# Moving the split of the second weights ahead of the next sum, and the first block's ELU ahead of a weight split, in a three-stage kernel on one core

## The chip, the cores and the metric

The kernel runs on one core of a Trainium2 chip. The metric is the device time of one execution in microseconds. Three executions of the kernel before took 698.92, 700.79 and 702.18 us, so the median is 700.79 us. The profile is of one more execution, of 699.52 us.

## The reference

Three stages follow each other. The first is an attention in which a query sees only the keys that fall to the same one of 16 centroids; there are 16 heads in all (2 batches of 8), 768 positions each. The second is a layer with an ELU between two products, for 1536 tokens. The third sends each token to one of eight experts. The change lies at the end of the first stage and in the second.

```python
def _moe_ref(x, w_in, w_out):            # x 1536 x 512, w_in 512 x 2048, w_out 2048 x 512
    h = x @ w_in
    g = np.where(h > 0.0, h, np.exp(np.minimum(h, 0.0)) - 1.0)
    return (g @ w_out).astype(np.float32)
```

## The kernel before

A product in full precision is made of three products of a reduced type: each operand is split into a head (names that end in H) and a rest (L), and head times head, rest times head and head times rest are summed in PSUM. For activations the head is a ScalarE copy and the rest a VectorE subtraction; for weights the head is a ScalarE copy (L705) and the rest a GpSimd subtraction (L706), both in `w_split`.

The weights of the second layer are taken as pairs of 32-bit words and rounded by a conversion, `round64`, one half of a 128 x 1024 tile `r` at a time. It is a generator whose steps are called from outside, one `next` each: ScalarE writes cv_a (L675) and then cv_t (L677), VectorE works cv_a (L679), cv_b (L681) and cv_b again (L684), and GpSimd sums cv_b and cv_t into r (L686). Half 0 of tile k holds first weights (w1), half 1 second weights (w2).

The second layer goes over the two batches, 16 steps each: k = 0 to 15 for the first batch, in which the weights are converted and also stored, and k = 16 to 31 for the second, in which they are read back. A step k has two blocks of hidden units times 384 tokens (part 0 and part 1, PSUM banks p and v). Each block takes twelve products on TensorE (L719, `ffn_h`): eight with w1H, then four with w1L. Then comes its ELU, `ffn_elu`, a generator of three steps: ScalarE makes two passes (L734, L735); VectorE one (L737) and ScalarE the head gH (L738); VectorE the rest gL (L740). Then come eighteen products with the second weights of the step before (L751, `ffn_second`): twelve with w2H and six with w2L. So step k needs r's half 1 of tile k - 1 (whose conversion began in step k - 1 as `high`), splits it into w2H and w2L, and prepares w1 of tile k + 1 (conversion `low`, begun in step k - 1).

The order on each engine is the order in which the code issues: the schedule is written out by hand, every engine works its own instructions strictly in that order, and semaphores join them. In a step the loop of `ffn` issues the end of `high` (a sum on GpSimd), the first block, the middle of `low` on VectorE, the first ELU's ScalarE passes, then the sum of `low` and the split of w2; later the second block, its ELU, and the split of w1 for the next step. In steps 9 to 14 GpSimd also finishes the last pair of heads, one piece per step (`side`: L501, L506 or L510).

The end of attention follows a written table, SCHEDULE, whose names W0 to W6 stand for parts of the second layer's step 0 that are put between the last pair's work: W0 to W3 issue three products each of the first block, W4 to W6 the three steps of its ELU (`elu[0]`). `early`, from `w_early`, is a generator of eleven steps that converts and splits the first weights of tiles 0 and 1; it is called after the last seven exponentials and at W0 to W3. Its last step sums r of tile 1 and splits it into w1H and w1L.

Of the kernel before, what the change touches and what calls it, by code (L numbers as in the profile page):

```python
# [65 lines left out]
class _Core:  # L66
# [446 lines left out]
    def steps(self):  # L513

        end = {}
        at = {"vtH": self.v_head, "vtL": self.v_rest, "loadqk": self.load_qk, "loadv": lambda n: self.load_nat(n + 1, "v"),
              "back": self.turn_back, "sv": self.similarities, "mx": self.largest, "eqsub": self.less_largest,
              "first": self.candidates, "least": self.first_of_them, "equal": self.one_hot, "rows": self.turn_one_hot,
              "oT": self.mask_rows}

        def put(at, name, f, *a):
            at[name] = lambda n: f(n, *a)
        for h in range(2):
            for nm in "qk":
                for x, f in (("turn", self.turn), ("TH", self.turn_head), ("raw", self.turn_raw), ("TL", self.turn_rest),
                             ("sim", self.similar)):
                    put(at, f"{x}{nm}{h}", f, nm, h)
            for name, f in (("back", self.turn_back), ("mx", self.largest), ("eqsub", self.less_largest),
                            ("first", self.candidates), ("least", self.first_of_them), ("equal", self.one_hot),
                            ("rows", self.turn_one_hot), ("oT", self.mask_rows)):  # L530
                put(at, f"{name}{h}", f, h)
            put(at, f"sT{h}", self.similar_out, h)
            put(at, f"moveT{h}", self.move_qk, h)
            put(at, f"moveO{h}", self.move_mask, h)
            for s in range(2 * self.NC):
                ab = "ab"[h]
                put(at, f"scores{s}{ab}", self.scores, s, h)
                put(at, f"flip{s}{ab}", self.flip, s, h)
                put(at, f"head{s}{ab}", self.head, s, h)
                put(at, f"rest{s}{ab}", self.rest, s, h)  # L540
        for s in range(2 * self.NC):
            put(at, f"peak{s}", self.peak, s)
            put(at, f"exp{s}", self.expo, s)
        for j in range(2 * self.NC // GU):
            for i in range(4):
                put(at, f"pv{j}{'abcd'[i]}", self.pv, j, i)
            put(at, f"pvlow{j}", self.pv_low, j)
            put(at, f"pvsum{j}", self.pv_sum, j)

        put(at, "invert", self.invert)  # L550
        for name, f in (("sumT", self.turn_sums), ("invrow", self.inverse_row), ("invdma", self.inverse)):
            put(end, name, f)
        for h in range(2):
            for x, f in (("mul", self.divide), ("xH", self.x_head), ("xL", self.x_rest)):
                put(end, f"{x}{h}", f, h)

        last = {}
        for i in range(4):
            put(last, f"W{i}", self.first_h, i)
        for i in range(4, 7):  # L560
            put(last, f"W{i}", lambda n: next(self.elu[0]))
        return at, end, last

    def first_h(self, n, i):

        self.ffn_h(0, 0, 3 * i, 3 * i + 3)
        next(self.early, None)

    def early_weights(self, u):
        NU, PER = self.B * self.H * self.NC, 2 * self.NC  # L570
# [189 lines left out]
    def ffn(self):  # L760

        NF = self.DFF // 128
        side = self.attention_rest()
        next(side)
        self.y, self.rest, low, high, routing = [], [], None, None, iter(())
        for k in range(2 * NF):
            if high:
                next(high, None)  # L770
            if k == 1:
                self.y.append(self.ffn_banks())
            if k == NF + 1:
                self.ffn_pools_after()
                routing = self.route_beside(0, self.y[0])
                next(routing)
                self.y.append(self.ffn_banks())
            if k:
                self.ffn_h(k, 0)
            if low:  # L780
                next(low)
                next(low)
                next(low)
            if k >= NF:
                self.w_split(k, 1)
                if k + 1 < 2 * NF:
                    self.w_split(k + 1, 0)
            elu, elu1 = self.elu[0] if k == 0 else self.ffn_elu(k, 0), self.ffn_elu(k, 1)
            next(elu, None)
            if low:  # L790
                next(low, None)
            if 0 < k <= NF:
                self.w_split(k - 1, 1)
            high = None
            if k < NF:
                high = self.round_half(k, 1)
                next(high)
            next(elu, None)
            self.ffn_h(k, 1)
            if high:  # L800
                next(high)
                next(high)
            next(elu, None)
            next(elu1)
            if high:
                next(high)
            if 0 < k < NF and k + 1 < 2 * NF:
                self.w_split(k + 1, 0)
            next(elu1)
            if high:  # L810
                next(high)
            next(elu1)
            low = None
            if k + 2 < NF:
                low = self.round_half(k + 2, 0)
                next(low)
                next(low)
            elif k + 2 < 2 * NF:
                self.w_load(k + 2)
            if k >= LATER:  # L820
                next(side, None)
            if k - NF in (4, 8):
                self.expert_load()
            ops = self.ffn_second(k - 1) if k else []
            for op in ops[:len(ops) // 2]:
                op()
            next(routing, None)
            for op in ops[len(ops) // 2:]:
                op()
            next(routing, None)  # L830
            if k:
                self.w_raw.pop(k - 1)
        self.drain(routing)
        for op in self.ffn_second(2 * NF - 1):
            op()
        self.rest.sort(key=lambda op: op[0])
# [555 lines left out]
```

## Time and profile before

| | |
|---|---|
| median of three executions | 700.79 us |
| the profiled execution | 699.52 us, span of the core 697.8 us |
| TensorE products busy | 666.6 us, 96% of the span |
| VectorE / ScalarE / GpSimd busy | 487.2 / 446.7 / 268.3 us |
| granted TensorE clock, mean | 0.984 of full speed |

The span is shorter than the execution's time by what lies before the first and after the last instruction. TensorE is busy for nearly the whole span, so most waits of the other engines cost nothing; what can be won on the way is the few gaps of TensorE. Busy shares of VectorE and GpSimd contain time in which an instruction has been issued and stands: an instruction's duration in a row runs from its issue to its end. In the timeline the start of an instruction can lie a little before the end of the one ahead of it on the same engine.

### The profile page before, as it was taken

The page shows a single profiled execution, that of the slowest core. Times are in us where ns is not written, and L with a number is a line of the kernel's source. Part 1 is how long each engine was busy: PE and PEld are TensorE (multiplying, and loading weights), DVE is VectorE, ACT ScalarE, POOL GpSimd, SP SyncE. Part 2 cuts the span into 40 slices and gives each one's busy share as a digit, 9 for nine tenths or more (in the row PEclk, how much of TensorE's full clock was granted, in tenths as well). Part 3 has the DMA queues.
Part 4 walks back from the last instruction along what each step waited for, and adds up shares of the span by engine and source line. Part 5 has one row for each costly group of instructions (what it writes and reads, how often), then busy time and mean ns, then how long its engine had stood idle before and what let it go on. Part 6 is the DMA issues. An engine that isn't in the chain of part 4 may idle for free. (4 is left out here: it accounts for less than half of the span.)

```text
span 697.8 us, 12196 instructions
## 1 busy us (share of the span) xinstructions
PE 666.6 (96%) x4272; PEld 608.7 (87%) x4272; DVE 487.2 (70%) x933; ACT 446.7 (64%) x968; POOL 268.3 (38%) x254
## 2 busy tenths in 40 slices
PE   5799999999999998999999999999999999999994
PEld 3699999999998887788888899999999898999994
DVE  5499998999999997999999852432364563226662
ACT  4499989899998987677767664445545312215551
POOL 1423446254545224666788752222243004022010
PEclk9699999999999999999999999999999999999998
DMA  7636657564664532655454446424110249989930
GB/s 174 156 77 141 157 130 162 127 142 114 152 141 102 126 116 62 210 192 192 168 195 161 172 173 214 160 73 166 62 61 16 91 172 378 339 290 316 354 141 13
DMA packets 73734, 111.41 MB, mean 160 GB/s; under 512 B 31105, under 2 KB 41441, under 8 KB 73664
## 3 DMA queue, kind: packets, MB, share of 16 engines
q1 hardware_dynamic: 70432, 106.07, 50.4%
q0 software_dynamic: 1488, 3.99, 1.6%
q8 instruction: 36, 0.59, 0.4%
q10 hardware_dynamic: 1744, 0.48, 0.3%
q14 instruction: 34, 0.28, 0.1%
HBM read 73.81 MB, written 16.92 MB: 130 GB/s over the span
## 5 line engine op out<-in xcount | busy, mean ns | idle before, releaser
L441 DVE TENSOR_TENSOR ptL<-ps_t,ptH 128x384 fp32r<-128x384 f32 x192 | 102.6, 551 | 10.4 <-ACT ptH L435 8.2
L435 ACT ACTIVATE ptH<-ps_t 128x384 fp32r<-128x384 f32 x192 | 91.2, 489 | 16.9 <-PE ps_t L423 12.8
L423 PE MATMUL ps_t<-ident,pe 128*128 128x128 f32 x576 | 94.3, 277 | 2.9 <-DVE ptL L441 2.2
L454 PE MATMUL ps_v<-ptH,vt 128*128 128x256 f32 x288 | 78.1, 295 | 0.0
L423 PEld LDWEIGHTS ps_t<-ident,pe 128*128 128x128 f32 x576 | 67.9, 141 | 11.6 <-DVE ptL L441 7.4
L454 PE MATMUL ps_v<-ptL,vt 128*128 128x256 f32 x288 | 77.2, 297 | 0.0
L706 POOL TENSOR_TENSOR w2L<-r,w2H 128x512 fp32r<-128x512 f32 x28 | 42.5, 1517 | 69.4 <-PE ps_t L751 62.2
L686 POOL TENSOR_TENSOR r<-cv_b,cv_t 128x512 int32<-128x512 int32 x32 | 43.1, 1346 | 44.6 <-DVE cv_b L684 24.2
L454 PEld LDWEIGHTS ps_v<-ptH,vt 128*128 128x128 f32 x288 | 54.0, 189 | 1.5
L454 PEld LDWEIGHTS ps_v<-ptL,vt 128*128 128x128 f32 x288 | 53.5, 190 | 0.2 <-DVE ptL L441 0.2
L407 DVE TENSOR_REDUCE st<-ps_sA 128x1 f32<-128x768 f32 x48 | 45.6, 949 | 8.4 <-PE ps_sA L401 8.0
L734 ACT ACTIVATE e<-ps_p 128x384 f32<-128x384 f32 x32 | 15.7, 490 | 55.7 <-PE ps_p L719 55.7
L407 DVE TENSOR_REDUCE st<-ps_sB 128x1 f32<-128x768 f32 x48 | 45.7, 952 | 4.3 <-PE ps_sB L401 4.2
L1197 POOL DMA_INDIRECT out_dram<-o,dest x10 | 11.5, 1155 | 92.1 <-DVE o L1195 91.5
L679 DVE SCALAR_TENSOR_TENSOR cv_a<-cv_a,d 128x512 f32<-128x512 f32 x32 | 44.3, 1383 | 3.5 <-ACT cv_a L675 3.3
L737 DVE SCALAR_TENSOR_TENSOR ps_p<-e,ps_p 128x384 f32<-128x384 f32 x32 | 17.9, 560 | 41.1 <-ACT e L735 41.1
L706 POOL TENSOR_TENSOR w1L<-r,w1H 128x512 fp32r<-128x512 f32 x32 | 44.1, 1379 | 6.4 <-ACT w1H L705 6.4
L414 ACT ACTIVATE pe<-ps_sA,st 128x768 f32<-128x768 f32 x48 | 43.3, 903 | 3.8 <-DVE st L407 3.8
L719 PE MATMUL ps_p<-xH,w1H 128*128 128x384 f32 x128 | 43.9, 343 | 2.0 <-DVE gL L740 2.0
L414 ACT ACTIVATE pe<-ps_sB,st 128x768 f32<-128x768 f32 x48 | 43.0, 897 | 0.5 <-DVE st L407 0.3
L719 PE MATMUL ps_p<-xL,w1H 128*128 128x384 f32 x128 | 42.9, 335 | 0.0
L719 PE MATMUL ps_v<-xL,w1H 128*128 128x384 f32 x124 | 41.4, 334 | 0.0
(378 smaller groups left out, 1930.8 us busy)
## 6 DMA issues: line engine op xcount, KB each, us to landing
ew<-in_moe_w_dram SPq DMA_DIRECT2D x32, 1024.0 KB, 7.6
d<-in_moe_w_in_dram SPq DMA_DIRECT2D x16, 512.0 KB, 4.0
d<-in_moe_w_out_dram SPq DMA_DIRECT2D x16, 512.0 KB, 4.1
wf_d<-r SPq DMA_DIRECT2D x16, 512.0 KB, 2.8
r<-wf_d SPq DMA_DIRECT2D x16, 512.0 KB, 3.3
KA<-kH SPq DMA_DIRECT2D x32, 192.0 KB, 3.7
natq<-in_q_dram SPq DMA_DIRECT2D x16, 192.0 KB, 3.8
natv<-in_v_dram SPq DMA_DIRECT2D x16, 192.0 KB, 3.9
```

Of the source, the lines that this page charges most:

```text
L407: self.nc.vector.tensor_reduce(st, self.sc[u][:, :, 0:384], axis=AX.XY, op=ALU.max, negate=True)
L414: self.nc.scalar.activation(pe, self.sc.pop(u)[:, :, 0:384], AF.Exp, bias=self.peaks.pop(u), accum_out=self.sums[n][:, s:s + 1])
L423: self.nc.tensor.transpose(ps[:, 0, j * 128:j * 128 + 128], self.pe[u][:, half, j * 128:j * 128 + 128], self.ident)
L435: self.nc.scalar.activation(self.split(u, half)[0], self.tp[u, half][:, 0, 0:384].rearrange("p (c q) -> p c q", c=3), AF.Copy)
L441: self.nc.vector.tensor_tensor(l, self.tp.pop((u, half))[:, 0, 0:384].rearrange("p (c q) -> p c q", c=3), h.bitcast(F32), ALU.subtract)
L454: self.nc.tensor.matmul(self.vp[n, j], lhsT=self.vt[n][:, j // NG, c, :], rhs=t, start=(part == 0 and i == 0), stop=(part == 3 and i == 2 ...
L679: V.scalar_tensor_tensor(a, a, LEAST_HI, hi.bitcast(F32), ALU.is_ge, ALU.mult)
L686: G.tensor_tensor(out.bitcast(I32), b, t, ALU.add)
L706: self.nc.gpsimd.tensor_tensor(l, x, h.bitcast(F32), ALU.subtract)
L719: self.nc.tensor.matmul(ps, lhsT=w[:, c, :], rhs=x[:, c, :], start=(i == 0), stop=(i == 11))
L734: S.activation(e, ps, AF.Relu, scale=-1.0)
L737: V.scalar_tensor_tensor(ps, e, -1.0, ps, ALU.add, ALU.max)
```

## The change

Two places are written in another order; no instruction is added or removed. In `ffn`, the split of w2 is issued ahead of the sum of `low`. At the end of attention, the last step of `early` (sum, w1H, w1L of tile 1) is called at W5, behind the first two steps of the first block's ELU, and no longer at W3.

```diff
         for i in range(4, 7):
-            put(last, f"W{i}", lambda n: next(self.elu[0]))
+            put(last, f"W{i}", self.first_elu, i)
         return at, end, last
 
     def first_h(self, n, i):
 
         self.ffn_h(0, 0, 3 * i, 3 * i + 3)
-        next(self.early, None)
+        if i < 3:
+            next(self.early, None)
+
+    def first_elu(self, n, i):
+        next(self.elu[0])
+        if i == 5:
+            next(self.early, None)
...
             elu, elu1 = self.elu[0] if k == 0 else self.ffn_elu(k, 0), self.ffn_elu(k, 1)
             next(elu, None)
+            if 0 < k <= NF:
+                self.w_split(k - 1, 1)
             if low:
                 next(low, None)
-            if 0 < k <= NF:
-                self.w_split(k - 1, 1)
```

GpSimd in two steps of the loop, before. `r` with cv_b and cv_t is a sum; of the two sums in a row the first belongs to second weights (half 1), the second to first weights (half 0).

```order
L686 TENSOR_TENSOR r_4070<-cv_b_4252,cv_t_4253 128x512
L686 TENSOR_TENSOR r_4289<-cv_b_4291,cv_t_4292 128x512
L706 TENSOR_TENSOR w2L_4340<-r_4070,w2H_4339 128x512
L706 TENSOR_TENSOR w1L_4372<-r_4289,w1H_4371 128x512
L686 TENSOR_TENSOR r_4211<-cv_b_4344,cv_t_4345 128x512
L686 TENSOR_TENSOR r_4381<-cv_b_4383,cv_t_4384 128x512
L706 TENSOR_TENSOR w2L_4432<-r_4211,w2H_4431 128x512
L706 TENSOR_TENSOR w1L_4464<-r_4381,w1H_4463 128x512
```

The same two steps now:

```order
L692 TENSOR_TENSOR r_4070<-cv_b_4252,cv_t_4253 128x512
L712 TENSOR_TENSOR w2L_4339<-r_4070,w2H_4338 128x512
L692 TENSOR_TENSOR r_4289<-cv_b_4291,cv_t_4292 128x512
L712 TENSOR_TENSOR w1L_4372<-r_4289,w1H_4371 128x512
L692 TENSOR_TENSOR r_4211<-cv_b_4344,cv_t_4345 128x512
L712 TENSOR_TENSOR w2L_4431<-r_4211,w2H_4430 128x512
L692 TENSOR_TENSOR r_4381<-cv_b_4383,cv_t_4384 128x512
L712 TENSOR_TENSOR w1L_4464<-r_4381,w1H_4463 128x512
```

In each step w2L and the sum of the next first weights have changed places; ScalarE and VectorE keep their order in the loop.

ScalarE at the end of attention, before. `ps_p` is the first block's bank, `xtmp` and `row` belong to the last pair of heads, `cv_a` begins the next conversion.

```order
L435 ACTIVATE ptH_4105<-ps_t1_4122 128x3x128
L705 ACTIVATE w1H_4140<-r_4070 128x512
L734 ACTIVATE e_4160<-ps_p_4091 128x384
L735 ACTIVATE e_4160<-e_4160 128x384
L738 ACTIVATE gH_4161<-ps_p_4091 128x384
L463 ACTIVATE xtmp_4167<-ps_v_4144 64x256
```

The same place now:

```order
L435 ACTIVATE ptH_4105<-ps_t1_4122 128x3x128
L740 ACTIVATE e_4155<-ps_p_4091 128x384
L741 ACTIVATE e_4155<-e_4155 128x384
L744 ACTIVATE gH_4156<-ps_p_4091 128x384
L711 ACTIVATE w1H_4163<-r_4070 128x512
L463 ACTIVATE xtmp_4167<-ps_v_4139 64x256
```

The three passes of the ELU stand ahead of w1H; the copy xtmp still comes last.

GpSimd at the same place, before, where `xH` and `xL` are the split of an attention result of the pair before the last:

```order
L706 TENSOR_TENSOR w1L_4048<-r_3859,w1H_4047 128x512
L686 TENSOR_TENSOR r_4070<-cv_b_4072,cv_t_4073 128x512
L706 TENSOR_TENSOR w1L_4141<-r_4070,w1H_4140 128x512
L506 CAST xH_175<-xr_3455 128x384
L510 TENSOR_TENSOR xL_176<-xr_3455,xH_175 128x384
L510 TENSOR_TENSOR xL_174<-xr_3455,xH_173 128x384
```

And now:

```order
L712 TENSOR_TENSOR w1L_4048<-r_3859,w1H_4047 128x512
L506 CAST xH_175<-xr_3455 128x384
L510 TENSOR_TENSOR xL_176<-xr_3455,xH_175 128x384
L692 TENSOR_TENSOR r_4070<-cv_b_4072,cv_t_4073 128x512
L712 TENSOR_TENSOR w1L_4164<-r_4070,w1H_4163 128x512
L510 TENSOR_TENSOR xL_174<-xr_3455,xH_173 128x384
```

The sum and w1L of tile 1 have gone behind one xH and one xL; the second xL stays behind them.

## Rows read from the trace of the kernel before

**Rows 1.** Busy time of TensorE by stretch: us, busy, instructions, clock, DMA.

```profile
410.00:690.00 280.00, 277.17 (x1761) 0.99 0.51 183
```

**Rows 2.** Timeline, TensorE's weight loads that waited: start, duration, form, idle before.

```profile
274.72 0.19 PEld L719 LDWEIGHTS ps_p<-xH,w1H 128*128 128x128 f32 x1 [2.27 <-ACT cv_a L675]
...
283.70 0.30 PEld L751 LDWEIGHTS ps_sA<-w2L,gH 128*128 128x128 f32 x2 [1.40 <-POOL w2L L706]
...
342.93 0.30 PEld L751 LDWEIGHTS ps_sA<-w2L,gH 128*128 128x128 f32 x2 [0.34 <-POOL w2L L706]
...
395.78 0.30 PEld L751 LDWEIGHTS ps_sA<-w2L,gH 128*128 128x128 f32 x2 [0.73 <-POOL w2L L706]
```

**Rows 3.** Timeline of TensorE, a step of the layer's second half.

```profile
499.55 0.33 PE L719 MATMUL ps_v<-xH,w1H 128*128 128x384 f32 x1
...
501.63 0.39 PE L751 MATMUL ps_sA<-w2H,gH 128*128 128x512 f32 x1
...
507.81 0.33 PE L719 MATMUL ps_v<-xH,w1H 128*128 128x384 f32 x1
```

**Rows 4.** Timeline, one step of the layer's first half.

```profile
311.81 0.71 PEld L719 LDWEIGHTS ps_p<-xH,w1L 128*128 128x128 f32 x4
...
313.50 0.75 DVE L684 SCALAR_TENSOR_TENSOR cv_b<-cv_a,top,cv_b 128x512 int32<-128x512 int32 x1
...
313.83 0.62 ACT L705 ACTIVATE w2H<-r 128x512 fp32r<-128x512 f32 x1
...
314.48 1.30 POOL L686 TENSOR_TENSOR r<-cv_b,cv_t 128x512 int32<-128x512 int32 x1 [2.10 <-ACT w2H L705]
...
315.04 1.29 DVE L679 SCALAR_TENSOR_TENSOR cv_a<-cv_a,d 128x512 f32<-128x512 f32 x1 [0.31 <-ACT cv_a L675]
...
315.74 1.75 POOL L706 TENSOR_TENSOR w2L<-r,w2H 128x512 fp32r<-128x512 f32 x1
...
316.72 1.05 DVE L681 TENSOR_SCALAR cv_b<-cv_a 128x512 int32<-128x512 int32 x1
...
317.47 1.45 POOL L706 TENSOR_TENSOR w1L<-r,w1H 128x512 fp32r<-128x512 f32 x1
...
317.69 0.55 DVE L737 SCALAR_TENSOR_TENSOR ps_v<-e,ps_v 128x384 f32<-128x384 f32 x1
...
318.16 1.31 DVE L684 SCALAR_TENSOR_TENSOR cv_b<-cv_a,top,cv_b 128x512 int32<-128x512 int32 x1
...
319.55 1.29 POOL L686 TENSOR_TENSOR r<-cv_b,cv_t 128x512 int32<-128x512 int32 x1 [0.63 <-DVE cv_b L684]
```

**Rows 5.** Timeline, the end of attention.

```profile
267.94 0.88 PE L719 MATMUL ps_p<-xH,w1L 128*128 128x384 f32 x4
...
269.18 1.28 POOL L686 TENSOR_TENSOR r<-cv_b,cv_t 128x512 int32<-128x512 int32 x1 [6.03 <-DVE cv_b L684]
...
270.49 0.63 ACT L705 ACTIVATE w1H<-r 128x512 fp32r<-128x512 f32 x1 [2.20 <-POOL r L686]
...
271.20 1.29 POOL L706 TENSOR_TENSOR w1L<-r,w1H 128x512 fp32r<-128x512 f32 x1 [0.74 <-ACT w1H L705]
...
273.20 0.38 ACT L463 ACTIVATE xtmp<-ps_v 64x256 f32<-64x256 f32 x1
```

**Rows 6.** Lines of GpSimd: shapes, count, busy us, mean ns, idle before.

```profile
L501 POOL TENSOR_TENSOR xr<-xr,inv 128x384 f32<-128x384 f32 x16 | 17.3, 1085 | 45.0 <-DMA inv<-inv_d 45.0
...
L506 POOL CAST xH<-xr 128x384 fp32r<-128x384 f32 x16 | 9.0, 564 | 0.0
```

**Rows 7.** Timeline, two close meetings of VectorE and GpSimd.

```profile
18.28 0.36 DVE L343 TENSOR_TENSOR oh<-eq,mn 128x192 bf16<-128x192 f32 x1
18.30 1.19 POOL L264 TENSOR_TENSOR qL<-raw,qH 128x384 fp32r<-128x384 f32 x1
...
362.91 1.28 POOL L686 TENSOR_TENSOR r<-cv_b,cv_t 128x512 int32<-128x512 int32 x1
362.96 1.78 DVE L679 SCALAR_TENSOR_TENSOR cv_a<-cv_a,d 128x512 f32<-128x512 f32 x1
```

## The prediction

> **What bounds the kernel now.** I read the page's busy shares first, then the waits of TensorE in the stretch that the change touches, then one step of that stretch engine by engine. From 410 us on TensorE is busy 277.17 of 280.00 us [rows 1], so a microsecond won or lost before that shows in full at the end. The stretch that the change touches is the first half of the second layer, the fifteen loop steps k = 1 to 15 from about 275 to 406 us. There TensorE stops once in each step, in front of the six products that read w2L [rows 2]. From 283.70 to 342.93 are seven steps, 8.46 us each; from 342.93 to 395.78 six steps, 8.81 us each [rows 2]. In the second half the same 42 products, with nothing late, take 8.26 us from 499.55 to 507.81 [rows 3]. So TensorE is only 0.20 and 0.55 us per step short of its own pace.
>
> What holds it is a chain of VectorE and GpSimd that take turns [rows 4]. GpSimd sums r at 314.48 to 315.78; VectorE's L679 starts at 315.04 and ends only at 316.33, 0.55 after GpSimd. GpSimd's w2L is issued at 315.74 and ends at 317.49, 1.16 after L679's end. L681 ends 0.28 after that (317.77), w1L 1.15 after L681 (318.92), L684 0.55 after w1L (319.47), and the next sum starts 0.08 later. Bare, w1L takes 1.29 [rows 5] and L684 0.75 [rows 4]. One of the two engines always stands until the other has finished; the passes that read PSUM (L737, 0.55) do not take part. The chain closes on itself in 8.46 us and TensorE waits on it.
>
> The Trainium skill, SBUF — State Buffer, Who interferes with whom, says that a VectorE instruction with two SBUF inputs and a GpSimd instruction that reads SBUF exclude each other for the whole instruction, the one issued first going first. The rows agree on the exclusion, but GpSimd's data starts about 0.12 us before VectorE's recorded end (1.16 against a bare 1.29), so not for the whole instruction; with two such handovers in the new chain below, holding it to the end would add 0.25 us per step, and the sum would be near zero instead of minus 1.4.
>
> **The change, part by part.** First the end of attention. In front of step 0 ScalarE stands 2.20 us until GpSimd's sum ends (269.18 + 1.28), and only after w1H (270.49 to 271.12) does it start the first block's ELU, although that block's last products were issued at 267.94 and were done by 268.82 [rows 5]. VectorE's xr pass and then the rest gL come behind ScalarE's copy at 273.20, and TensorE restarts at 274.72, after 2.27 us of idle weight load [rows 2, 5]. With the ELU ahead of w1H, its passes fill the 2.20 us. Between w1H's end and the copy 2.08 us of ELU go away (273.20 minus 271.12); w1H itself comes about 0.47 later, since gH of the ELU ends near 271.06 by my addition of the same passes. That leaves 2.08 - 0.47 = 1.6 us. What is late next is the same chain (w1H, copy, VectorE, gL), so not all of the 2.27 goes. GpSimd does one xH and one xL earlier, in the time in which it waited for the sum; these are read only in the second half of the layer. Term: -1.6, with 0 and -2.2 as ends.
>
> Second, the first w2L. At 283.70 TensorE had waited 1.40 us for it [rows 2]. With w2L ahead of the sum it is started once w2H is there, two microseconds or so earlier: -1.3. But TensorE then meets w1L of the next step, which now stands behind w2L and the sum; by the same durations that gives 0.6 back at once. Together -0.7.
>
> Third, the steady step. w2L needs w2H, which ends at 314.45, and the sum r started at 314.48 [rows 4]: so w2L takes the sum's slot, ends near 315.8, and TensorE's wait for it is gone. But the sum now ends where w2L ended, near 317.5; w1H, which on ScalarE reads that sum and started 0.7 earlier before, comes behind it, and w1L behind w1H. Call the end of the sum R. VectorE's L681, held back by the sum, ends at R + 0.28, L737 follows, and L684 is issued at R + 0.67 (318.16 against 317.49 [rows 4]). ScalarE starts w1H 0.03 after the sum, takes 0.63, and GpSimd issues w1L 0.08 later (270.46, 270.49, 271.20 [rows 5]): R + 0.74. L684 is 0.07 us ahead. Taking it first, L684 runs its bare 0.75 to R + 1.42, and w1L ends 1.15 later, at R + 2.57. Now TensorE waits for w1L, in the middle of its first block. The new cycle: w1L to TensorE 0.05; from the first w1L load (311.81) to w2H's end 2.64; w2L 0.08 + 1.29; L679 0.55; sum 1.16; to w1L's end 2.57. Sum 8.34, against 8.46: -0.12 in each of seven steps, -0.8. TensorE's own 8.26 is the lower end.
>
> Fourth, the six steps from 342.93 in which GpSimd also does a piece of the last pair (L501 or L510, about 1.0 us, or the cast L506 at 0.5 [rows 6]). There the sum of the other half comes late, and w2H with it. The cycle: L679 0.55, the extra piece 0.9, L681 0.28, sum 1.16, w2H 0.66, w2L 1.37, L679 0.55, sum 1.16, to w1L's end 2.57: 9.2 us, or 8.7 with a cast. Mean (4 x 9.2 + 2 x 8.7) / 6 = 9.03 against 8.81: +0.22 x 6 = +1.3. Before, the piece was paid only in part, because w2L stood last in the chain. In the last step w1L is late once more: +0.2. Step 0 itself has the same order as the others but costs nothing new: its sum waits for VectorE, not for GpSimd's place.
>
> Sum: -1.6 - 0.7 - 0.8 + 1.3 + 0.2 = -1.6; the second xL now runs beside VectorE's L679 of step 0, which takes 0.2 back (the xr and L679 passes follow each other there), so -1.4. Against the profiled execution's own 699.52 us that is 698.1. The median shown is 700.79, 1.27 above that execution, so I forecast 699.4.
>
> **The rivals.** A second outcome: GpSimd goes first at that meeting. The 0.07 us is less than the 0.08 by which VectorE issues an instruction before the one ahead of it has ended (318.16 against 317.69 + 0.55 [rows 4]). Two close meetings in the trace went by issue: at 18.28 VectorE, 0.02 ahead, ran its 0.36 and GpSimd's took 1.19; at 362.91 GpSimd, 0.05 ahead, ran its 1.28 and VectorE's took 1.78 [rows 7]. But at neither was a VectorE instruction, issued over its predecessor, ahead. If w1L wins, L684 ends 1.16 later; the sum behind it and the first two passes of the next conversion slide, and the next step's L684 of the first half is then issued after w2L and stands behind it. That delays L737, gH, ScalarE's second ELU and so w1H. TensorE waits for w1H at the head of the block. The cycle: w1H to TensorE 0.06, a block of twelve 2.08 [rows 3], result and the two ELU passes and w2H about 2.05, w2L 1.4, L684 0.55, L737 0.5, then six ScalarE passes (gH, the conversion's second pass, the second ELU's two, w1H) about 2.5: 9.1 us. Each of seven steps then costs +0.62, or +4.3; the steps with extra pieces about +2, the first w2L gives back 0.9 instead of 0.6: in all +4.7, 705.5 us. It decides from the moment that w1L is issued, or served, 0.07 us earlier against L684, and once in that state the order holds itself, since both then follow from ScalarE. For it: the smallness of the lead. Against it: both meetings above.
>
> A third outcome: the chain has more slack than I give it, w1L does not hold TensorE, and the steps go at TensorE's pace: -0.20 x 7 - 0.55 x 6 - 1.4 - 1.6 = -7.7 at the utmost, and half of that, 697, as a likely size. For it: the 8.46 before held about 0.6 us in which neither engine used its turn. Against it: four GpSimd and six VectorE passes add up to 7.8 us per step and 8.8 with an extra piece, so the latter cannot go below what they take now.
>
> A fourth: a part of the gain does not come through, because the copy at 273.20 still sets gL, or because in the new order GpSimd starts its data at VectorE's recorded end and not 0.12 us ahead of it; the rest stands as forecast: about 701. For the second speaks only the page quoted above, against it each handover in [rows 4].
>
> **How the numbers follow.** Chances: forecast 0.52 (its own range 697.6 to 701.2), GpSimd first 0.31, TensorE's pace 0.11, fourth 0.06. What a measurement of this kernel can tell from no change is about 0.5%, 3.5 us: faster means below 697.3, slower above 704.3. Faster: the third outcome and the forecast's edge, 0.13. Slower: the second but for its low edge, and an edge of the first, 0.31. Same: 0.56. The range reaches from 696.5, which takes in half of the third, to 706.3, the top of the second.
>
> **What would show it.** In the changed profile TensorE's waits for w2L should be gone; in their place stand short waits (near 0.1 us) for w1L within the first block and a step of 8.3 to 8.4 us before the extra pieces, 9.1 to 9.2 with them. L684 of the second half must take 0.75 and w1L 1.8. If instead L684 takes 1.76 and w1L 1.29, TensorE waits for w1H and the step is 9.1, the second outcome. TensorE's restart after the first two blocks should come at about 273.1 instead of 274.72. A step of 8.26 throughout, or a step above 9.3, would make the prediction wrong in its mechanism.

## The result, and the profile after

The changed kernel takes 704.34 us (median of six executions, 703.06 to 705.73); the kernel before takes 700.50 us in the same comparison. The ratio is 1.0056 with a 95% interval of 1.0037 to 1.0075: slower, where 699.4 us and no difference were forecast. The execution profiled is of 703.93 us, with a span of 702.2 us. The change sets every line from 671 on six lower in the file: L684 is now L690, L686 is L692, L706 is L712, L705 is L711, L719 is L725, L737 is L743.

From 414 us on TensorE is as busy as before, so the loss lies ahead of that, as [rows 1] let expect (columns as there; the further ones are the other engines):

```profile
414.00:690.00 276.00, 273.75 (x1745) 251.92 (x1744) 124.22 (x336) 119.75 (x261) 60.76 (x51) 1.00 0.52 186
```

The end of attention went as worked out. The timeline of the changed kernel there, which answers to [rows 5]:

```profile
268.10 0.86 PE L725 MATMUL ps_p<-xH,w1L 128*128 128x384 f32 x4
...
270.67 0.49 ACT L744 ACTIVATE gH<-ps_p 128x384 fp32r<-128x384 f32 x1 [0.63 <-DVE ps_p L743]
...
271.06 0.62 ACT L711 ACTIVATE w1H<-r 128x512 fp32r<-128x512 f32 x1
...
271.71 0.38 ACT L463 ACTIVATE xtmp<-ps_v 64x256 f32<-64x256 f32 x1
```

The ELU's last ScalarE pass is done before w1H, and the copy xtmp comes 1.49 us earlier (273.20 before). TensorE restarts at 273.23; from the first block's last products that is 5.13 us, where it was 274.72 - 267.94 = 6.78. So 1.65 us is gained, with 1.6 forecast.

The loss is in the loop. TensorE's loads that waited (timeline of the changed kernel, weight loads; they answer to [rows 2]):

```profile
273.23 0.19 PEld L725 LDWEIGHTS ps_p<-xH,w1H 128*128 128x128 f32 x1 [0.63 <-ACT cv_a L681]
278.73 0.19 PEld L757 LDWEIGHTS ps_sA<-w2H,gH 128*128 128x128 f32 x1 [1.39 <-ACT w2H L711]
283.65 0.19 PEld L725 LDWEIGHTS ps_p<-xH,w1H 128*128 128x128 f32 x1 [0.97 <-ACT w1H L711]
...
304.22 0.19 PEld L725 LDWEIGHTS ps_v<-xH,w1H 128*128 128x128 f32 x1 [0.35 <-DVE gL L746]
310.90 0.19 PEld L725 LDWEIGHTS ps_p<-xH,w1H 128*128 128x128 f32 x1 [0.65 <-ACT w1H L711]
313.29 0.19 PEld L725 LDWEIGHTS ps_v<-xH,w1H 128*128 128x128 f32 x1 [0.34 <-DVE gL L746]
```

The waits for w2L are gone. In their place TensorE waits twice in each step, for w1H at the head of the first block and for gL ahead of the second, and from 304.22 to 313.29 a step is 9.07 us. The lengths of all fifteen steps, each from the first load of one second block (k = 1 to 15) to that of the next, from the same view of both kernels:

```
before   10.37 | 8.46 8.47 8.47 8.44 8.46 8.46 8.47 | 8.85 8.88 8.68 8.70 8.89 8.87 | 8.25
changed  10.79 | 9.08 9.10 9.07 9.07 9.08 9.07 9.07 | 9.24 9.15 8.66 8.66 9.15 9.17 | 8.26
sums: +0.42, +4.31 for the seven steps, +1.16 for the six with an extra piece, +0.01
```

In all +5.90; less the 1.65 at the restart that is +4.25, and the two spans differ by 4.4 (the other 0.15 lie ahead of the restart). The seven steps without an extra piece are the loss. One of them on VectorE, ScalarE and GpSimd (timeline of the changed kernel, which answers to [rows 4], and above it the loop's first step):

```profile
278.75 1.29 POOL L712 TENSOR_TENSOR w2L<-r,w2H 128x512 fp32r<-128x512 f32 x1 [1.09 <-ACT w2H L711]
278.78 1.81 DVE L690 SCALAR_TENSOR_TENSOR cv_b<-cv_a,top,cv_b 128x512 int32<-128x512 int32 x1
...
310.93 1.29 POOL L712 TENSOR_TENSOR w1L<-r,w1H 128x512 fp32r<-128x512 f32 x1 [1.72 <-ACT w1H L711]
310.95 1.82 DVE L690 SCALAR_TENSOR_TENSOR cv_b<-cv_a,top,cv_b 128x512 int32<-128x512 int32 x1
...
314.97 1.41 POOL L712 TENSOR_TENSOR w2L<-r,w2H 128x512 fp32r<-128x512 f32 x1 [0.83 <-ACT w2H L711]
315.26 1.67 DVE L690 SCALAR_TENSOR_TENSOR cv_b<-cv_a,top,cv_b 128x512 int32<-128x512 int32 x1
316.85 0.55 DVE L743 SCALAR_TENSOR_TENSOR ps_p<-e,ps_p 128x384 f32<-128x384 f32 x1
...
317.43 0.49 ACT L744 ACTIVATE gH<-ps_p 128x384 fp32r<-128x384 f32 x1 [1.97 <-DVE ps_p L743]
...
319.31 0.61 ACT L711 ACTIVATE w1H<-r 128x512 fp32r<-128x512 f32 x1
```

A meeting is a place in the step where a pass of GpSimd and one of VectorE come close; if they overlap, one stands until the other is nearly through. Each step has two, and GpSimd wins both. At 310.93 w1L is 0.02 us ahead of the second half's L690, which takes 1.82. At 314.97 w2L is 0.29 ahead of the first half's L690, which takes 1.67. Behind that one stands L743 and, through it, ScalarE, which idles 1.97 us before gH and gets to w1H only at 319.31. This is the second outcome of the prediction, with its signature: L690 near 1.8 at the w1L meeting, w1L 1.29, a wait for w1H, 9.1 us per step. What the prediction did not see is at the top of the fence: in the loop's first step w2L was issued 0.03 us ahead of the first half's L690, and the order is there from then on until the extra pieces begin.

### The profile page after: what moved, and what is told of

Same layout as the page of the kernel before. It is cut to its first block, busy times and chain, and to the rows that moved or that the text cites. A ratio compares the mean times of both kernels' runs of the same rounds, so it can differ in the third digit from the quotient of the medians.

```text
span 702.2 us, 12182 instructions
## 1 busy us (share of the span) xinstructions
PE 669.8 (95%) x4272; PEld 607.0 (86%) x4272; DVE 492.6 (70%) x933; ACT 448.3 (64%) x968; POOL 266.8 (38%) x254
## 5 line engine op out<-in xcount | busy, mean ns | idle before, releaser
L712 POOL TENSOR_TENSOR w2L<-r,w2H 128x512 fp32r<-128x512 f32 x28 | 37.1, 1325 | 80.0 <-PE ps_t L757 62.1
L712 POOL TENSOR_TENSOR w1L<-r,w1H 128x512 fp32r<-128x512 f32 x32 | 44.9, 1403 | 25.0 <-ACT w1H L711 25.0
L692 POOL TENSOR_TENSOR r<-cv_b,cv_t 128x512 int32<-128x512 int32 x32 | 45.3, 1416 | 21.3 <-DVE cv_b L690 16.9
L725 PE MATMUL ps_p<-xH,w1H 128*128 128x384 f32 x128 | 44.7, 349 | 2.6 <-ACT w1H L711 2.2
L690 DVE SCALAR_TENSOR_TENSOR cv_b<-cv_a,top,cv_b 128x512 int32<-128x512 int32 x32 | 45.5, 1422 | 0.5
L685 DVE SCALAR_TENSOR_TENSOR cv_a<-cv_a,d 128x512 f32<-128x512 f32 x32 | 43.9, 1373 | 2.5 <-ACT cv_a L681 2.5
L743 DVE SCALAR_TENSOR_TENSOR ps_p<-e,ps_p 128x384 f32<-128x384 f32 x32 | 17.8, 557 | 39.3 <-ACT e L741 39.3
L725 PE MATMUL ps_p<-xL,w1H 128*128 128x384 f32 x128 | 42.9, 335 | 0.0
```

The source lines that it names most:

```text
L685: V.scalar_tensor_tensor(a, a, LEAST_HI, hi.bitcast(F32), ALU.is_ge, ALU.mult)
L690: V.scalar_tensor_tensor(b, a.bitcast(I32), self.top2, b, ALU.bitwise_and, ALU.bitwise_or)
L692: G.tensor_tensor(out.bitcast(I32), b, t, ALU.add)
L712: self.nc.gpsimd.tensor_tensor(l, x, h.bitcast(F32), ALU.subtract)
L725: self.nc.tensor.matmul(ps, lhsT=w[:, c, :], rhs=x[:, c, :], start=(i == 0), stop=(i == 11))
L743: V.scalar_tensor_tensor(ps, e, -1.0, ps, ALU.add, ALU.max)
```

## The experiments

My theory at this point: the loop has two orders that hold themselves, one of 8.3 us per step in which VectorE's L690 goes first at both meetings (VectorE's order below) and one of 9.07 in which GpSimd does (GpSimd's order), and the close meeting of the first step chooses. (It is close, but falls the same way each time: w2L, or the first piece of it, is issued 0.01 to 0.04 us ahead there in every trace of a kernel with the swap.) Its rivals: the new order is slower in any case; or the ELU's move, not the swap, does it; or, as the prediction had it, the meeting of w1L with L690 chooses. Step lengths below are k = 1 to 15, taken as above, with | around the six extra-piece steps; ratios are to the kernel before in the same comparison.

**ELU move alone** (the two statements of `ffn` back in the old order).

```diff
-            if 0 < k <= NF:
-                self.w_split(k - 1, 1)
             if low:
                 next(low, None)
+            if 0 < k <= NF:
+                self.w_split(k - 1, 1)
```

> The ELU's move alone, the split of the second weights left where it was. Theory (two separate terms, the loss is in the loop): TensorE restarts after the first two blocks 1.6 us earlier than before, the loop keeps its 8.46 us steps, about 698.9 us against 700.5 before. Rival (the earlier start also shifts the engines of the loop against each other and costs there): steps other than 8.46 us, 700.5 us or more.

698.52 us, ratio 0.9985 (0.9972 to 0.9998). Steps 10.87, 8.46 8.49 8.47 8.47 8.46 8.47 8.47 | 8.87 8.85 8.72 8.70 8.85 8.85 | 8.26: the old steps, so the loss isn't the ELU's. TensorE restarts 5.15 us after the first block's last products (271.70 against 266.55), 1.63 less than before. Yet the gain is 1.0 us, since the first step is 0.50 longer: the wait for w2H has grown. The second xL is now issued just 0.01 us ahead of VectorE's next conversion pass (L685, L679 before), which stands behind it and takes 1.54 instead of 1.03; L687, L743, ScalarE's passes and w2H come later by it. Timelines, this kernel and then the one before:

```profile
271.49 1.01 POOL L510 TENSOR_TENSOR xL<-xr,xH 128x384 fp32r<-128x384 f32 x1
271.50 1.54 DVE L685 SCALAR_TENSOR_TENSOR cv_a<-cv_a,d 128x512 f32<-128x512 f32 x1
...
277.19 0.19 PEld L757 LDWEIGHTS ps_sA<-w2H,gH 128*128 128x128 f32 x1 [1.35 <-ACT w2H L711]
```

```profile
274.53 1.03 DVE L679 SCALAR_TENSOR_TENSOR cv_a<-cv_a,d 128x512 f32<-128x512 f32 x1
...
279.71 0.19 PEld L751 LDWEIGHTS ps_sA<-w2H,gH 128*128 128x128 f32 x1 [0.87 <-ACT w2H L705]
```

**Swap in the loop alone** (the kernel before with the two statements of `ffn` in the new order).

```diff
+            if 0 < k <= NF:
+                self.w_split(k - 1, 1)
             if low:
                 next(low, None)
-            if 0 < k <= NF:
-                self.w_split(k - 1, 1)
```

> The split of the second weights ahead of the sum alone, the ELU left where it was. Theory (the new order has two states, and the meeting of w2L with VectorE's L684 in step 1 decides; here too GpSimd is issued some 0.03 us ahead): steps 2 to 8 take 9.07 us, about 705.9 us. Rival (the slow state comes only with the ELU's shift): steps of 8.34 us, about 700.5 us.

704.91 us, ratio 1.0082 (1.0064 to 1.0100). Steps 9.82, 9.08 9.07 9.08 9.07 9.07 9.08 9.06 | 9.24 9.15 8.65 8.66 9.17 9.18 | 8.26. The swap makes the loss by itself. (The 9.82 is no gain of 0.55: in this execution the granted clock was 0.50, the lower of its two levels, from 276 to 278 us and 0.67 in the 2 us before, so the block ahead of the count took 2.49 instead of 2.02. From TensorE's restart to the second step's second block it is 12.31 us here and 12.39 before.) Its first meeting (timeline) is closer still, and GpSimd wins again:

```profile
278.27 1.29 POOL L706 TENSOR_TENSOR w2L<-r,w2H 128x512 fp32r<-128x512 f32 x1 [1.11 <-ACT w2H L705]
278.28 1.84 DVE L684 SCALAR_TENSOR_TENSOR cv_b<-cv_a,top,cv_b 128x512 int32<-128x512 int32 x1
```

**The first w2L in two pieces** (the changed kernel; only the loop's first w2L is cut, into 64 and 448 columns, so that L690 waits for the short piece alone).

```diff
-        self.nc.gpsimd.tensor_tensor(l, x, h.bitcast(F32), ALU.subtract)
+        for s in ((slice(0, 64), slice(64, 512)) if (k, j) == (0, 1) else (slice(0, 512),)):
+            self.nc.gpsimd.tensor_tensor(l[:, s], x[:, s], h[:, s].bitcast(F32), ALU.subtract)
```

> As the changed kernel, but the one GpSimd subtraction for w2L in step 1 is issued in two pieces, 64 and 448 columns, so that VectorE gets its turn between them. Theory (a meeting lost by 0.03 us in step 1 sets the state of the whole loop): steps 2 to 8 take 8.34 us instead of 9.07, those from 9 on as in the changed kernel; 704.3 - 7 x 0.73 = 699.2 us. Rival (the order itself costs 9.07 us per step): no change, 704.3 us within 0.3.

697.07 us, ratio 0.9969 (0.9954 to 0.9983). Steps 10.37, 8.28 8.28 8.28 8.29 8.30 8.28 8.28 | 9.16 9.18 8.65 8.66 9.18 9.18 | 8.27. One instruction of the whole program is cut, and seven steps lose 0.8 us each; 699.2 us was expected. In the timeline L690 takes 0.84 in the first step, and four steps later, with nothing cut, VectorE goes first at both meetings:

```profile
277.44 1.88 POOL L713 TENSOR_TENSOR w2L<-r,w2H 128x64 fp32r<-128x64 f32 x2 [1.08 <-ACT w2H L711]
277.47 0.84 DVE L690 SCALAR_TENSOR_TENSOR cv_b<-cv_a,top,cv_b 128x512 int32<-128x512 int32 x1
...
310.47 0.75 DVE L690 SCALAR_TENSOR_TENSOR cv_b<-cv_a,top,cv_b 128x512 int32<-128x512 int32 x1
...
311.18 1.29 POOL L713 TENSOR_TENSOR w2L<-r,w2H 128x512 fp32r<-128x512 f32 x1 [1.02 <-ACT w2H L711]
...
314.84 0.74 DVE L690 SCALAR_TENSOR_TENSOR cv_b<-cv_a,top,cv_b 128x512 int32<-128x512 int32 x1
314.91 1.83 POOL L713 TENSOR_TENSOR w1L<-r,w1H 128x512 fp32r<-128x512 f32 x1 [0.74 <-ACT w1H L711]
```

The lead of L690 over w1L is 0.07 us here, as forecast, and its lead over w2L 0.71. So the new order isn't slower in any case.

**One w1L in two pieces, in the fourth step** (the changed kernel, same edit with `(k, j) == (5, 0)`).

> As the changed kernel, but the one GpSimd subtraction for w1L in step 4 is issued in two pieces, 64 and 448 columns. Theory (the state can be left at any step by turning one meeting round): steps 2 to 4 stay at 9.07 us, steps from 5 to 8 take 8.34; 704.3 - 4 x 0.73 = 701.4 us. Rival (the state is fixed by the start of the loop, or by the order): 9.07 us throughout, 704.3 us.

700.56 us, ratio 1.0021 (1.0008 to 1.0034). Steps 10.76, 9.09 9.09 9.28 8.29 8.29 8.28 8.28 | 9.18 9.16 8.67 8.64 9.17 9.18 | 8.28. GpSimd's order is left in the middle of the loop and doesn't come back. In the timeline the cut lets L690 through at 310.30 (0.85), the next L690 of a first half is 0.69 ahead of w2L, and so on without a cut:

```profile
310.27 1.89 POOL L713 TENSOR_TENSOR w1L<-r,w1H 128x64 fp32r<-128x64 f32 x2 [1.71 <-ACT w1H L711]
310.30 0.85 DVE L690 SCALAR_TENSOR_TENSOR cv_b<-cv_a,top,cv_b 128x512 int32<-128x512 int32 x1
...
314.18 0.75 DVE L690 SCALAR_TENSOR_TENSOR cv_b<-cv_a,top,cv_b 128x512 int32<-128x512 int32 x1
...
314.87 1.30 POOL L713 TENSOR_TENSOR w2L<-r,w2H 128x512 fp32r<-128x512 f32 x1 [1.01 <-ACT w2H L711]
```

**Three tries to enter GpSimd's order, by a memset.** All three start from the kernel with the first w2L in two pieces and put one VectorE memset ahead of one L690 in the fifth step (`late` is true there alone), to make it the later one: 128 x 64 and 128 x 256 at the w1L meeting, 128 x 1024 at the w2L meeting.

```diff
+        if late:
+            V.memset(self.spare, 0.0)
```

> The kernel with w2L of step 1 in two pieces, which runs at 8.28 us per step, plus one small VectorE memset (128 x 64) in front of the L684 pass that meets w1L in step 5, so that this pass is issued some 0.1 us later, behind w1L, which it led by 0.07. Theory (two states that hold themselves; one turned meeting changes over): steps from 6 to 8 take 9.07 us, 697.1 + 3 x 0.79 = 699.5 us. Rival (the fast state is the stable one and comes back after one step): at most one longer step, 697.1 to 698.0 us.

> The kernel with w2L of step 1 in two pieces (8.28 us per step), plus a VectorE memset of 128 x 256 in front of the L684 pass that meets w1L in step 5, enough to put it behind w1L once; in the run before, with a quarter of it, VectorE still got its turn first. Theory A (any lost meeting changes the state): the steps after the one with the memset take 9.07 us up to step 8, in all some +2.4 us. Theory B (the meeting with w1L alone does not enter the slow state; what does is w2L going ahead of the first half's L684, which delays L737 and all that ScalarE does behind it): one step of about 8.75 us, then 8.28 again, in all +0.5 us.

> The same kernel, with a VectorE memset of 128 x 1024 in front of the first half's L684 in step 5 instead, enough (over 0.7 us) to put it behind w2L once. Theory B (w2L ahead of that L684 enters the slow state, which then holds itself): one step of about 9.3 us, then three of 9.07 up to step 8, then the steps with extra pieces as ever; in all 1.0 + 3 x 0.79 = +3.4 us or a little more for the memset. Theory C (a stall on VectorE is paid once and the fast order comes back): one longer step of up to 9.3 us, then 8.28 again, in all +1.0 us.

696.12, 695.74 and 696.42 us, ratios 0.9959 (0.9942 to 0.9977), 0.9975 (0.9963 to 0.9987) and 0.9981 (0.9965 to 0.9997). No meeting was turned: one step of 8.48 with the second, one of 9.00 with the third, all others 8.3. So these runs don't tell the theories apart; the third shows only that L693, ended 0.8 us later within its step, costs one step and no more when GpSimd does not go first. Timelines of the second and the third, where L693 is what L690 is above:

```profile
314.83 2.03 POOL L716 TENSOR_TENSOR w1L<-r,w1H 128x512 fp32r<-128x512 f32 x1 [0.74 <-ACT w1H L714]
314.89 0.27 DVE L692 MEMSET spare<- 128x256 f32 x1
315.09 0.62 DVE L693 SCALAR_TENSOR_TENSOR cv_b<-cv_a,top,cv_b 128x512 int32<-128x512 int32 x1
```

```profile
311.06 0.91 DVE L692 MEMSET spare<- 128x1024 f32 x1 [0.16 <-issue]
311.64 2.03 POOL L716 TENSOR_TENSOR w2L<-r,w2H 128x512 fp32r<-128x512 f32 x1 [1.03 <-ACT w2H L714]
311.90 0.62 DVE L693 SCALAR_TENSOR_TENSOR cv_b<-cv_a,top,cv_b 128x512 int32<-128x512 int32 x1
```

GpSimd was issued 0.26 us ahead of L693 in both and still went second: 2.03 is its bare 1.29 and 0.74 of standing, which reaches to 0.14 us before L693's end.

**w1L first, once** (same base; in place of the memset one VectorE maximum over a PSUM bank).

```diff
+        if late:
+            V.tensor_reduce(self.spare, self.hps[5, 1], axis=AX.X, op=ALU.max)
```

> The kernel with the first w2L in two pieces (its steps are 8.28 us), and one VectorE pass more, once, in step 5: a maximum over one PSUM bank, ahead of the L684 of the second half. Unlike the memsets, which ran in the shared turn and kept it for the L684 behind them, a pass that reads PSUM does not take part in the turns (the 0.55 us L737 before), so it should put L684 some 0.4 us behind w1L and turn that one meeting: w1L near 1.3 us, L684 of that step 1.2 to 1.8. Theory (two orders that hold themselves; the meeting that decides between them is that of w2L with the L684 of the first half, not that of w1L with the L684 of the second): one step of 8.6 to 8.9 us, then 8.28 again, total about 0.5 us above the kernel with the first w2L in two pieces, about 697.5 where that has 697. Rival, the one of the prediction as it was written (w1L first against L684 of the second half is enough, and then holds itself): steps of 9.07 from there to step 8, three of them, +2.5 to 3 us.

698.82 us, ratio 1.0005 (0.9989 to 1.0020). Steps 10.36, 8.32 8.32 8.31 8.31 8.67 8.34 8.35 | 9.11 9.17 8.67 8.64 9.17 9.19 | 8.31. This meeting was turned (timeline):

```profile
316.77 1.30 POOL L716 TENSOR_TENSOR w1L<-r,w1H 128x512 fp32r<-128x512 f32 x1 [0.74 <-ACT w1H L714]
317.34 0.56 DVE L692 TENSOR_REDUCE spare<-ps_v 128x1 f32<-128x384 f32 x1 [0.56 <-ACT gH L748]
317.81 0.81 DVE L693 SCALAR_TENSOR_TENSOR cv_b<-cv_a,top,cv_b 128x512 int32<-128x512 int32 x1
...
321.10 0.75 DVE L693 SCALAR_TENSOR_TENSOR cv_b<-cv_a,top,cv_b 128x512 int32<-128x512 int32 x1
321.32 1.70 POOL L716 TENSOR_TENSOR w2L<-r,w2H 128x512 fp32r<-128x512 f32 x1 [1.33 <-ACT w2H L714]
```

w1L ran its 1.30 unhindered and L693 ended at 318.62, 2.60 us behind the sum's end (314.27 + 1.75); the prediction's addition for a w1L that goes first gives R + 2.58, so the delay is the one that the second outcome spoke of. The next L693 is still 0.22 ahead of w2L (0.71 without the edit), and the step after is 8.34. So the w1L meeting alone does not lead into GpSimd's order: the rival fails in the form in which the prediction had it. (In this kernel and the next two the other steps ahead of the extra pieces are 0.03 to 0.05 longer, and in the layer's second half, where nothing is edited, a step takes 8.31 instead of 8.25, which makes 0.8 us there; about 1 us of the whole time remains beside that. What makes them longer stays open. Their spare tile has 1 or 385 columns, that of the memset kernels, without the effect, 64, 256 or 1024; whether it is this was not tested.)

**w2L first, once.** A first try put two maxima over the first block's PSUM bank ahead of a first half's L690.

> As the run before it, but two PSUM maxima ahead of the L684 of the first half in step 5, some 0.8 us, so that w2L is issued first at that meeting, as it was by 0.025 us in step 1 of the changed kernel. Theory (this meeting decides, and each order holds itself): one step of 9.1 to 9.4 us, then 9.07 each until the extra pieces begin with step 9, in all 3 to 3.5 us above the kernel with the first w2L in two pieces, about 700.3. Rival (the chain has one order that it falls back to, and the change's loss came from its first steps alone): the delay is paid once, one step of 8.8 to 9.3 and then 8.28 again, at most +1.0 us, about 698.

700.52 us, ratio 1.0020 (1.0007 to 1.0033), one step of 10.24 and the others up to step 8 of 8.3: ScalarE's pass on the same bank waited for the maxima, so w2L itself came about 2 us late and nothing was turned. Inconclusive. The second try takes them over an SBUF tile that nobody else uses:

```diff
+        if late:
+            for _ in range(2):
+                V.tensor_reduce(self.spare[:, 384:385], self.spare[:, 0:384], axis=AX.X, op=ALU.max)
```

> The kernel with the first w2L in two pieces (steps of 8.28 us), and in step 5 two VectorE maxima over an SBUF tile of 128x384, ahead of the L684 of the first half; the maxima over PSUM had made ScalarE's first ELU pass wait, which reads the same bank, and so w2L itself came late. Here nothing else reads the tile. They should put that L684 some 0.9 us later, 0.2 us or more behind w2L, so that w2L is issued first, as it was by 0.025 us in step 1 of the changed kernel. Theory (this meeting decides, and each order holds itself): one step of 8.8 to 9.4 us, then 9.07 each until the extra pieces begin with step 9; in all 2.5 to 3.5 us above the kernel with the first w2L in two pieces. Rival (the chain falls back to one order, and the change's loss came from its first steps alone): one step of 8.8 to 9.3 and then 8.28 again, at most +1.0 us. Should the maxima over SBUF keep the turn as the memsets did, the meeting is not turned and neither is told apart.

703.14 us, ratio 1.0044 (1.0026 to 1.0062). Steps 10.34, 8.35 8.33 8.32 **9.32 9.08 9.09 9.10** | 9.24 9.17 8.66 8.66 9.17 9.18 | 8.30. Here the meeting was turned, and GpSimd's order stays until the extra pieces begin (timeline; L695 is the L690 from above):

```profile
311.39 1.13 DVE L694 TENSOR_REDUCE spare<-spare 128x1 f32<-128x384 f32 x2
312.24 1.29 POOL L718 TENSOR_TENSOR w2L<-r,w2H 128x512 fp32r<-128x512 f32 x1 [1.05 <-ACT w2H L716]
312.44 1.65 DVE L695 SCALAR_TENSOR_TENSOR cv_b<-cv_a,top,cv_b 128x512 int32<-128x512 int32 x1
...
317.17 1.30 POOL L718 TENSOR_TENSOR w1L<-r,w1H 128x512 fp32r<-128x512 f32 x1 [1.72 <-ACT w1H L716]
317.19 1.83 DVE L695 SCALAR_TENSOR_TENSOR cv_b<-cv_a,top,cv_b 128x512 int32<-128x512 int32 x1
...
321.21 1.40 POOL L718 TENSOR_TENSOR w2L<-r,w2H 128x512 fp32r<-128x512 f32 x1 [0.83 <-ACT w2H L716]
321.50 1.66 DVE L695 SCALAR_TENSOR_TENSOR cv_b<-cv_a,top,cv_b 128x512 int32<-128x512 int32 x1
```

The delayed L695 was let in 0.20 us behind w2L; from then on w1L leads by 0.02 and w2L by 0.29, the very leads of the changed kernel. The four steps cost 3.5 us against 8.28 each. The maxima themselves also make L695 1.1 us later, so this run alone doesn't part the lost meeting from the longer stall; the first step of the changed kernel against that of the kernel with the cut, where nothing is put ahead of L690 and only the meeting differs, does. Together with the first-step cut the theory is shown from both sides: turned once at the w2L meeting, the loop changes its order and keeps it until the extra pieces begin.

**The better version** (first w2L cut, and the old order from the first step with an extra piece on).

```diff
-            if 0 < k <= NF:
+            if 0 < k <= LATER:
                 self.w_split(k - 1, 1)
             if low:
                 next(low, None)
+            if LATER < k <= NF:
+                self.w_split(k - 1, 1)
```

> The changed kernel with w2L of step 1 issued in two pieces (as in the run before, 697.1 us), but from step 9 on, where GpSimd has an extra piece in each step, the split of the second weights stands behind the sum again as before the change. Theory (in those six steps the new order is the slower one, by the chain of turns): six steps of 8.85 and 8.70 us instead of 9.17 and 8.65, 697.1 - 1.2 = 695.9 us, against 699.5 before. Rival (the extra pieces cost the same in either order): 697.1 us.

695.78 us, ratio 0.9958 (0.9943 to 0.9974), faster than both kernels. Steps 10.36, 8.28 8.30 8.29 8.29 8.28 8.29 8.28 | 9.33 8.85 8.72 8.68 8.89 8.86 | 8.25. Against the cut alone its steps are 0.7 us less in all, where 1.2 was expected (the first one in the old order takes 9.33 instead of 8.85); the intervals of the two ratios overlap, so that part rests on the traces.

## Why the prediction was wrong

The step that failed is the third part, the steady step, in what it took for granted: that the loop comes to that step in the order in which it was worked out. Seven steps that were to gain 0.12 us each lost 0.62 each. The working of the step itself was right. In the kernel with one w2L cut, L690 is 0.07 us ahead of w1L, takes 0.74 and w1L 1.83, and a step is 8.28 us (8.34 forecast); TensorE waits 0.05 to 0.07 for w1L there. Its own pace of 8.26 [rows 3] is so near that the third outcome fails by the six steps with extra pieces rather than by these. But what the loop repeats is handed to it by its first step. That step stands in the second part, where only TensorE's wait for w2L was costed; VectorE's L690 of the first half, which w2L meets there 0.03 us ahead, was not followed. It could have been read from the kernel before (timeline, its first loop step):

```profile
279.04 0.62 ACT L705 ACTIVATE w2H<-r 128x512 fp32r<-128x512 f32 x1
...
279.77 0.75 DVE L684 SCALAR_TENSOR_TENSOR cv_b<-cv_a,top,cv_b 128x512 int32<-128x512 int32 x1
```

The head w2H ends at 279.66, and with the 0.08 that the prediction itself gives between it and w2L, w2L moved ahead of the sum comes at 279.74, 0.03 ahead of L684. The 0.31 given to the second outcome went by the closeness of the wrong meeting: the lead at w1L is small but held in every run that had it, and losing it once (w1L first, once) costs 0.4 us and no more.

Point by point. The ELU's move: 1.65 us at the restart (1.6 forecast), but 0.50 comes back in the next step as a longer wait for w2H; the prediction's term for the second xL, which does this, was 0.2. The first w2L: its wait went, as forecast; but the first step is as long as before with the cut (10.37) and 0.42 longer in the changed kernel. Less the 0.50 of the xL, that leaves 0.5 won with the cut and 0.1 as made, in place of 0.7. The seven steady steps: -0.12 each forecast, -0.18 with the cut, +0.62 in the changed kernel; the second outcome had +0.62. The six steps with an extra piece: 9.2 and 8.7 forecast, 9.18 and 8.66 measured on average, +1.16 in all against +1.3; the second outcome's 2 us there was too much, since from the first extra piece on the changed kernel's steps are those of the kernel with the cut. The last step's +0.2 did not come (+0.01). With the cut, the restart's 1.65 and the steps' differences (0, -1.24, +1.14, +0.02) sum to -1.7; the forecast was -1.4, and that kernel measured -2.4 by the medians. So the forecast describes the change with one meeting turned, and the second outcome, +4.7 forecast and +3.8 measured, the change as it was made. In it, which meeting decides was wrong, and the price of the extra steps. The fourth outcome is out on both counts: the restart's gain came, and with the cut w1L ends 1.16 us behind L690's end (1.15 in the forecast). Its 701 us was too low besides: 0.25 us in each of the seven steps alone makes it up, and the other six have such handovers too.

Why does each order hold itself? Read from the rows above: if w2L goes first, L690 and with it L743, gH and w1H come late; then w1L and the second half's L690 both follow ScalarE, 0.02 us apart, L690 ends late again, and so the next first half's L690 is 0.29 behind w2L. Giving L690 the w1L meeting once moves it about 1 us against w2L (0.29 behind to 0.69 ahead), enough to get out. Taking that meeting from it in VectorE's order moves it 0.5 us (0.71 ahead to 0.22), not enough to get in.

## What to carry to other kernels

Where two engines take turns and each one's next start hangs on the other's end, don't cost a step only in its steady form: list every pair of their passes that can meet, with the lead of each, and follow them from the loop's first step, because one meeting lost by hundredths of a microsecond there may be repeated in every step. When a loop runs slower than its own sum, look at the step in which it first does, and try to turn that one meeting (here by cutting one instruction in two) before giving up the order.

## What the runs showed of the hardware

A few hundredths of a microsecond decided 6 us (the sum of the fifteen steps, changed kernel against the one with the first w2L cut): single passes that met went by issue at leads of 0.01 to 0.03 us (278.27 against 278.28, 278.75 against 278.78). But a VectorE pass right behind a memset went ahead of a GpSimd pass issued 0.26 us before it, and a memset issued 0.06 us behind GpSimd ran its 0.27 at once. Why a memset is treated otherwise stays open. That it takes the turn, as one expectation put it, is not shown: GpSimd's pass issued during the memset at 311.06 stood, but the memset at 314.89 did not wait for GpSimd's. A maximum over SBUF or PSUM let GpSimd through: w2L, issued during the two maxima at 312.24, ran its bare 1.29. The Trainium skill, SBUF — State Buffer, Who interferes with whom, says of trn2 that such a reduction never contends, and these rows agree; it also says that the order of issue decides who blocks, which the rows with the memset contradict.
